# Filtered spectrum sums and half copies over two frequency pairs at a time, in a newly searched order

## The chip, the cores and the metric

One core of one Trainium2 chip. The metric is the device time of one launch in microseconds (us), as the median of several runs. A ratio is the mean time of one kernel's fast runs over that of the other's fast runs of the same rounds, with a 95% interval, so it is not quite the ratio of the medians quoted beside it. The profile of a run gives a span (first to last instruction of the core) about 2 us shorter than its time. Differences under 0.5 us are read from the spans of all runs, not from the times.

## The reference, cut to what matters

```python
def reference(A_x, A_w_r, A_w_i, B_x, B_w_gate, B_w_up, B_w_down):
    xn = layernorm(A_x)                       # 2048 x 640
    y  = irfft2(rfft2(xn) * (A_w_r + 1j * A_w_i))
    g  = xn @ B_w_gate; u = xn @ B_w_up       # 640 -> 1536
    return A_x + y + (g * u) @ B_w_down       # 1536 -> 640
```

(B_x is not used.) Two independent branches are computed from the same normed input: a two-dimensional spectral filter, and a gated product. The second is mostly TensorE work; the first has much small work on VectorE and ScalarE.

## The kernel before

The kernel is a list of about a thousand tasks with what they read and write. A table found by a search (`_PLAN`) says for each task its place in the order, its engine, and its bank in PSUM. The engines then run their own lists, each in that fixed order, and wait on semaphores where a task needs another's result. Five parts matter here: `GU` (gate and up matmuls, five of 128x512 each) with its eviction `eG` and product `H`, and the steps `t = 0..15` of the filter, two frequencies in each:

```python
# C_t: forward product, TensorE, two PSUM banks. In the plan every C from C_1 on has banks 0 and 1.
# WM_t: multiply with the filter, VectorE, reads C's banks and frees them (4 x 256, 2 x 130 columns)
def em_sm(c, pb=pb, yr=yr):                       # SM_t: sums, VectorE
    pa_, pb_ = v_pr[:, pb, 0], v_pr[:, pb, 1]
    c.e.tensor_tensor(v_l[0:64, yr, :, 0, :], pa_[0:64], pb_[64:128], _OP.subtract)
    return c.e.tensor_tensor(v_l[64:128, yr, :, 0, :], pa_[64:128], pb_[0:64], _OP.add)
def em_ja(c, yr=yr):                              # JA_t, JB_t: half copies, VectorE or ScalarE
    return copy_on(c, v_l[0:64, yr, :, 1, :], v_l[64:128, yr, :, 0, :])
def em_jb(c, yr=yr):
    dst, src = v_l[64:128, yr, :, 1, :], v_l[0:64, yr, :, 0, :]
    ...                                           # the same with the sign turned
# IA_2t, IA_2t+1: inverse product, TensorE, reads v_l; eIA: its eviction
```

Before the filter steps the other half transform runs beside the first GUs; after them come `I` (second inverse transform), `V` (combining it, VectorE), `ACC` (down projection, 128x320 matmuls) and `IV` (the last transform, into ACC's bank). In what follows a "forward product" is a C, a "filter" a WM, an "inverse product" an IA.

## Time and profile before

| | before |
|---|---|
| time, first reading | 206.17 us (206.08 to 206.24) |
| time beside the changed kernel | 206.12 us |
| span in the profile | 204.0 us |
| busy: TensorE, VectorE, ScalarE | 195.5, 185.5, 134.9 us |
| middle stretch (73.0 to 136.2 us): VectorE busy | 60.7 of 63.2 us |

The lines behind it are shown in the prediction. One reading matters for all that follows: VectorE's busy time leaves 2.5 us of the middle stretch, but it has 180 instructions there, so this is 14 ns at each seam (the step from one instruction to the next). Its longest gap is 0.1 us, and its list of waits is empty: it never waits. A stretch in which an engine shows such seams only is filled by that engine.

### The profile page before, as it was taken

To read this page: it belongs to the slowest core of one execution; us is meant where nothing else is said; L and a number is where in the kernel's file an instruction comes from. 1 tells how busy PE (TensorE), PEld (TensorE's weight loads), DVE (VectorE), ACT (ScalarE), POOL (GpSimd) and SP (SyncE) were. 2 spreads that over 40 slices of the span, in tenths; PEclk is the share of its full clock that TensorE was granted. 3 is DMA by queue.
4 is the path that set the end of the run, shared out by engine and by line. 5 is a ranking of instruction groups with operands and counts; after the bars stand their busy time and mean duration, and the time that the engine had idled before them with its cause. 6 is when DMAs were issued, how large, how long until landed. Compare 5 with 4: busy or idle time off the path is not lost.

```text
span 204.0 us, 4331 instructions
## 1 busy us (share of the span) xinstructions
PE 195.5 (96%) x1623; PEld 123.4 (60%) x1623; DVE 185.5 (91%) x430; ACT 134.9 (66%) x297; POOL 22.9 (11%) x53
## 2 busy tenths in 40 slices
PE   7999999999999999989898988989999999999995
PEld 7898545455454554554454445467666777777774
DVE  3799999999999999999999999998999988989823
ACT  3288999989965799888989896677314414041331
POOL 0000000000000023433250423530000000000000
PEclk9999999999999999999999999999999999999999
DMA  6999956455049143142542320025002413315432
GB/s 185 304 335 385 373 66 129 120 123 131 16 86 332 45 101 92 46 125 52 146 115 62 86 67 0 0 62 166 3 0 69 124 35 96 96 35 158 133 100 64
DMA packets 29668, 23.79 MB, mean 117 GB/s; under 512 B 10576, under 2 KB 27600, under 8 KB 29520
## 3 DMA queue, kind: packets, MB, share of 16 engines
q1 hardware_dynamic: 28848, 23.16, 40.8%
q10 hardware_dynamic: 800, 0.36, 0.6%
q8 instruction: 13, 0.21, 0.5%
q14 instruction: 7, 0.06, 0.1%
HBM read 18.92 MB, written 2.62 MB: 106 GB/s over the span
## 4 chain that ended last, share of the span: by engine, by line
PE 67%; DVE 27%; issue 3%; POOL 1%; ACT 0%; POOLq 0%; DVEq 0%
PE ps L1222 26%; PE ps L951 24%; DVE arena L1065 10%; PE ps L971 7%; DVE arena L688 4%; DVE arena L987 3%; DVE arena L1071 3%; DVE arena L1081 3%; DVE arena L1080 3%; PE ps L911 2%; PE ps L1145 2%; PE ps L723 2%; PE ps L1234 2%; DVE arena L1092 2%; PE ps L821 1%
## 5 line engine op out<-in xcount | busy, mean ns | idle before, releaser
L687 ACT ACTIVATE arena<-ps 64x321 bf16<-64x321 f32 (+7 forms) x241 | 114.6, 522 | 57.6 <-PE ps L1234 30.2
L951 PE MATMUL ps<-arena 128*128 128x512 bf16 x420 | 98.8, 379 | 0.9 <-DVE arena L987 0.9
L951 PEld LDWEIGHTS ps<-arena 128*128 128x128 bf16 x420 | 38.4, 97 | 41.3 <-ACT arena L687 2.6
L1222 PE MATMUL ps<-arena 128*128 128x320 bf16 (+2 forms) x396 | 57.1, 295 | 0.0
L1222 PEld LDWEIGHTS ps<-arena 128*128 128x128 bf16 x396 | 37.7, 98 | 13.7
L1065 DVE TENSOR_TENSOR arena<-ps,arena 128x256 bf16<-128x256 f32 x64 | 22.6, 416 | 0.4
L1100 POOL COPY arena<-arena 128x126 bf16<-128x126 bf16 x16 | 6.5, 404 | 112.2 <-DVE arena L1071 112.2
L987 DVE TENSOR_TENSOR arena<-arena 128x512 bf16<-128x512 bf16 x42 | 17.7, 422 | 0.6
L971 PE MATMUL ps<-arena 128*128 128x128 bf16 (+1 forms) x160 | 14.0, 246 | 0.3 <-ACT arena L778 0.3
L971 PEld LDWEIGHTS ps<-arena 128*128 128x128 bf16 x160 | 12.2, 98 | 1.5 <-issue 0.4
L1261 DVE TENSOR_TENSOR arena<-arena 128x640 bf16<-128x640 bf16 x15 | 7.2, 486 | 5.8 <-ACT arena L687 5.7
L1114 PEld LDWEIGHTS ps<-arena 128*128 128x128 bf16 x128 | 7.8, 119 | 5.6 <-ACT arena L687 2.3
L1102 POOL TENSOR_SCALAR arena<-arena 128x130 bf16<-128x130 bf16 x16 | 10.8, 674 | 0.0
L1114 PE MATMUL ps<-arena 128*128 128x64 bf16 x128 | 8.5, 198 | 1.3 <-POOL arena L1102 0.6
L1028 PEld LDWEIGHTS ps<-arena 128*128 128x128 bf16 x160 | 7.0, 98 | 4.2 <-DVE arena L688 0.9
L1048 PE MATMUL ps<-arena 128*128 128x321 bf16 x32 | 7.0, 301 | 2.5 <-DVE arena L1071 2.5
L688 DVE CAST arena<-ps 128x512 bf16<-128x512 f32 (+3 forms) x15 | 8.7, 609 | 0.2
L750 ACT ACTIVATE arena<-arena 128x640 bf16<-128x640 bf16 x10 | 8.4, 838 | 0.1
L1234 PE MATMUL ps<-arena 128*128 128x320 bf16 (+2 forms) x33 | 8.4, 295 | 0.0
L1028 PE MATMUL ps<-arena 128*128 128x64 bf16 (+1 forms) x160 | 8.0, 193 | 0.1
L1071 DVE TENSOR_TENSOR arena<-ps,arena 128x130 bf16<-128x130 f32 x32 | 8.0, 292 | 0.0
L863 DVE TENSOR_TENSOR arena<-arena 128x768 f32<-128x768 bf16 (+1 forms) x10 | 7.9, 788 | 0.0
(66 smaller groups left out, 211.3 us busy)
## 6 DMA issues: line engine op xcount, KB each, us to landing
arena<-in_A_x_dram SPq DMA_DIRECT2D x20, 160.0 KB, 2.5
arena<-in_A_w_r_dram SPq DMA_DIRECT2D x30, 80.2 KB, 2.2
arena<-in_A_w_i_dram SPq DMA_DIRECT2D x30, 80.2 KB, 2.2
out_dram<-arena SPq DMA_DIRECT2D x15, 160.0 KB, 1.8
arena<-in_B_w_gate_dram SPq DMA_DIRECT2D x4, 320.0 KB, 5.4
arena<-in_A_x_dram SPq DMA_DIRECT2D x1, 1280.0 KB, 10.0
arena<-c_tf SPq DMA_DIRECT2D x4, 256.0 KB, 10.2
arena<-c_ti SPq DMA_DIRECT2D x2, 512.0 KB, 4.9
```

What stands on the lines that cost most here:

```text
L687: return c.e.activation(dst, src, _ACTF.Copy)
L688: return c.e.tensor_copy(dst, src)
L951: ins = c.e.matmul(ps[:, bk, :], v_gw[:, w, j, ft, :], v_xt[:, j, rows], start=(j == 0), stop=(j == 4))
L971: ins = c.e.matmul(ps[:, bk, w * n:(w + 1) * n], v_gw[:, w, j, ft, :], v_xt[:, j, rows], start=(j == 0), stop=(j == 4))
L987: return c.e.tensor_tensor(v_ht[:, ft0, rows], v_gbf[:, rr, 0, :], v_gbf[:, rr, 1, :], _OP.mult)
L1028: ins = c.e.matmul(ps[:, bk, k * 64:k * 64 + n], v_uq[:, k, t, :], v_fd[:, k * 128 + w * n: k * 128 + w * n + n], start=True, stop=True)
L1065: c.e.tensor_tensor(dst, xh, wv, _OP.mult)
L1071: ins = c.e.tensor_tensor(d5[w], ps[:, bk:bk + 2, 256:321], wt[:, w, :, 0:321:5], _OP.mult)
L1102: return c.e.tensor_scalar(yg[:, :, 128:193], yg[:, :, 256:321], -1.0, None, _OP.mult)
L1114: c.e.matmul(ps[:, bk, 64 * k:64 * k + 64], yl[:, k:512:4], v_ti[:, q, 0, :], start=True, stop=True)
L1222: ins = c.e.matmul(ps[:, bk, 0:sl3.stop - sl3.start], v_ht[:, ft, a * 128:(a + 1) * 128], v_wd[:, ft, sl3], start=(ft == _FT_ORDER[0]), st ...
L1234: return c.e.matmul(ps[:, bank_of(own), 0:sl3.stop - sl3.start], v_sm[:, 2, :], v_v[:, a, sl3], start=False, stop=True)
```

## The change

The intent is to halve the number of small VectorE instructions: sums and half copies are made over two steps (four frequencies) at once, so that the fixed cost of an instruction is paid half as often. The planner's durations for these tasks were set higher, and the whole order was searched again. The core of the diff (the plan, all of whose lines change, is cut):

```diff
-        b_pr = alloc("PR", 2 * 1024)
-        b_l = alloc("L", _NY * 1024)
+        b_pr = alloc("PR", 2048)
+        b_l = alloc("L", 2 * 2048)
...
-            wm = T("WM_%d" % t, "dve", 4 * _d_dve(256) + 2 * _d_dve(130), em_wm,
+            wm = T("WM_%d" % t, "dve", 1862.0, em_wm,
...
+            if t % 2 == 0:
+                continue
+            lr = (t // 2) % 2
+            def em_sm(c, lr=lr):
+                pa_, pb_ = v_pr[:, 0], v_pr[:, 1]
+                c.e.tensor_tensor(v_l[0:64, lr, :, 0, :], pa_[0:64], pb_[64:128], _OP.subtract)
+                return c.e.tensor_tensor(v_l[64:128, lr, :, 0, :], pa_[64:128], pb_[0:64], _OP.add)
...
-            for g in range(2):
-                q = 2 * t + g
+            for q in range(2 * t - 2, 2 * t + 2):
```

## The prediction

> **What bounds the kernel now.** I read the page first, then the chain of waits in order of time, then the busy times of each engine over three stretches, then the groups of instructions with shapes kept apart, and last the waits of the middle stretch.
>
> The page says that two engines are nearly full all the time, and where each of them is not.
>
> ```profile
> PE 195.5 (96%) x1623; PEld 123.4 (60%) x1623; DVE 185.5 (91%) x430; ACT 134.9 (66%) x297; POOL 22.9 (11%) x53
> PE   7999999999999999989898988989999999999995
> DVE  3799999999999999999999999998999988989823
> ACT  3288999989965799888989896677314414041331
> ```
>
> TensorE drops to 8 in slices 17 to 25 only, that is from about 80 to 130 us. In that region the chain of waits leaves TensorE and stays on VectorE:
>
> ```profile
> 70.63 0.59 PE ps L1028 x15
> ...
> 73.03 1.32 DVE arena L1065 x4
> 74.35 0.42 DVE arena L1071 x2
> 74.77 0.34 DVE arena L987
> 75.13 0.42 DVE arena L1080
> 75.57 0.42 DVE arena L1081
> 76.02 1.42 DVE arena L1065 x4
> 77.44 0.43 DVE arena L1071 x2
> 77.88 0.29 DVE arena L688
> 78.20 0.30 DVE arena L1092
> ```
>
> The reader is to see one task after the other with no hole: the filter products of one pair of frequencies (L1065 four times, L1071 twice, 1.85 us together), a gated product (L987), the sums (L1080 and L1081, each 0.44 us from start to start), and the two half copies (L688 and L1092, 0.32 us from start to start). This goes on until 135.5 us. Before 73 and after 136 the chain is TensorE alone.
>
> ```profile
> 1.04:73.03 71.99, 71.71 (x549) 44.24 (x550) 68.31 (x156) 58.26 (x129) 0.00 (x0) 1.00 0.69 190
> 73.03:136.23 63.20, 58.34 (x548) 31.47 (x546) 60.70 (x180) 54.90 (x123) 22.59 (x48) 1.00 0.27 68
> 136.23:201.75 65.52, 65.48 (x534) 47.64 (x531) 56.02 (x95) 21.76 (x47) 0.00 (x0) 1.00 0.29 88
> ```
>
> The columns are the stretch, its length, then busy time of PE, PE weight load, DVE, ACT and POOL. Only in the middle one is TensorE open, for 4.9 us by this count. The count flatters it, since matmul spans overlap. Worked out from distances in the trace (five 128x512 matmuls take 1.08 us, fifteen of L1028 take 0.59, a group of six of L1114 and L1116 takes 0.20, a 320-column one 0.136), the middle holds 190 x 0.216 + 135 x 0.039 + 32 x 0.20 + 30 x 0.136 = 56.8 us of streaming in 63.2 us: 6.4 us open. The last stretch by the same count holds 65.3 us in 65.5.
>
> So the most that a change of the middle stage can give is about 6.4 us, 3.1% of 206.17.
>
> **What the Trainium skill says.** "VectorE: DVE Perf Modes", section "The TRN2 errata", says that an instruction from SBUF pays a fixed latency once, however large it is. Its section "Side-by-side: where the cycles go" gives two 16-bit elements a cycle to a two-source operation and four to a copy, at 0.96 GHz: 0.52 and 0.26 ns an element. The trace agrees roughly:
>
> ```profile
> L987 DVE TENSOR_TENSOR arena<-arena 128x512 bf16<-128x512 bf16 x42 | 17.7, 422 | 0.6
> L988 DVE TENSOR_TENSOR arena<-arena 128x256 bf16<-128x256 bf16 x4 | 1.1, 270 | 0.0
> L1261 DVE TENSOR_TENSOR arena<-arena 128x640 bf16<-128x640 bf16 x15 | 7.2, 486 | 5.8 <-ACT arena L687 5.7
> L688 DVE COPY arena<-arena 64x512 bf16<-64x512 bf16 x14 | 4.2, 299 | 0.4
> ```
>
> From 256 to 512 elements is 152 ns (0.59 each), from 512 to 640 is 64 ns (0.50); some 150 ns is fixed. "TensorE: Matmul & The Clock Gate", section "Back-to-back issue gap", gives N/2.4 + 2.5 ns, 216 at 512, which is the distance above; the 131 ns that it also gives does not occur here. "Perfetto Trace Analysis", section "Identifying the Most-Contended Engine", warns that matmul busy time is no measure of headroom; here it reads 58.3 where the streaming is 56.8.
>
> **The change part by part.** I call the work of two frequencies a step; the stage has 16.
>
> Sums. Before: 32 instructions of 512 elements at 0.44 us, 14.1 us. After: 16 of 1024. One should last 422 + 512 x 0.55 = 0.70 us, 0.72 from start to start: 11.5 us. Saved: 2.6 us.
>
> Half copies. Before, 27 on VectorE at 0.32 us (8.6 us) and 5 on ScalarE at 0.63. After, the order of instructions shows 13 on VectorE and 3 on ScalarE. One on VectorE should last 299 + 512 x 0.26 = 0.43, 0.45 with its gap: 5.9 us. Saved: 2.7 us. The three on ScalarE should take about 1.05 each (the 512-element one takes 0.63; I add the page's rate of 0.83 ns per element), 3.2 us as before.
>
> Filter products: unchanged, 16 x 1.85 = 29.6 us.
>
> Moved by the new order: in the stage VectorE gets two more evictions of 320 columns (+1.0), one more gated product (+0.44), and loses one double eviction of 64x321 (-1.0). Net +0.4.
>
> VectorE in the stage: 62.5 - 2.6 - 2.7 + 0.4 = 57.6 us. Had TensorE room, this would be the gain: 5 us.
>
> TensorE's work is the same in kind and number, only in another order. Between the first L1048 and the end of the inverse transforms the new order has 205 gate and up matmuls of 512 where the old one had 190, and 10 of the down projection where it had none: 56.8 + 15 x 0.216 + 10 x 0.136 = 61.4 us. So the author knew that VectorE no longer fills the stage and put TensorE work there that was done later; the last stretch falls from 65.3 to about 60 us of streaming. ScalarE: five more 512-column evictions at some 0.55 and one less of 320, so 54.9 + 2.3 = 57.2 us.
>
> The stage therefore has 61.4 us on TensorE, 57.6 on VectorE, 57 on ScalarE. TensorE becomes the bound, and the gain is 6.4 us less what stays open on it. In the stretch up to 73 us three engines are as full (71.7, 68.3 and 58.3 of 72.0) and TensorE keeps no hole, so a good order can do it. In the stage the waits go round a loop (evict, transform, filter, sum, copy, transform back, evict), so I expect 2.3 us to stay open, under 4%. The last stretch gets tight: by my count from the rows of before, the first combined group of the inverse is ready about 14.3 us after the last inverse transform, and TensorE arrives at its first use at 13.9 to 14.3; the third is ready at 38.1 against 38.0 to 38.4. I take off 0.6 us for that and for the seams. Gain: 6.4 - 2.3 - 0.6 = 3.5 us, so 202.6 us.
>
> **The rivals.** First, a wait for four spectra takes the place of the wait for two. The inverse transform of a step now waits for the filter of the next one, one sum and two copies: 1.85 + 1.44 + 0.9 = 4.2 us later at worst. If TensorE has too little other work in its fixed order, or the buffer of the fifth products (three deep, held longer) stalls the filter, the stage keeps 4 to 6 us open and the gain is 0 to 2 us: 204 to 206. Against it: the order puts 3 to 5 us of TensorE work behind each last forward product, and 5 us behind the very last.
>
> Second, VectorE's gain comes out whole and TensorE keeps under 1 us open, as in the first stretch: 200.7 to 201.5. For it speaks that six waits fall away: of the old chain 2.5 us are TensorE's forward product waiting for the filter to give its two banks back, since all steps after the first used the same pair of banks, and the new order spreads them over four pairs.
>
> ```profile
> PE ps L1048 <- DVE arena L1071: 2.5, 7, 0.6
> PEld ps L1114 <- ACT arena L687: 2.3, 4, 0.7
> ```
>
> Third, ScalarE becomes the bound, at 57 of some 63 us with evictions that hold banks: its row of the second line above shows 2.3 us of TensorE waiting for it already. If that doubles, the time is about 204.
>
> **Range and chances.** The middle of the three is 202.6. Two us open less gives 201, two more gives 204.4; I take 201.0 to 204.4 for 8 in 10. Faster by over 2% needs 202.05, a gain of 4.1 of the possible 6.4 us, so under 2.3 us lost in all: 0.36. Slower by 2% would need a deadlock-like stall in every step: 0.02. The rest, 0.62, is within 2%.
>
> **What would show it right or wrong.** Right: the sums at 0.69 to 0.72 us and 16 of them, the copies at 0.42 to 0.45, the chain of the middle no longer VectorE without a break but mixed with long runs of L951; TensorE's open time there down from 6.4 to 2 to 3 us; the first and last stretches without new holes. Wrong: sums over 0.8 us; TensorE waiting over 4 us for ScalarE, POOL or the copies in the middle; or a last stretch in which TensorE waits for the combining of the inverse.

## The result, and the profile after

The changed kernel takes 199.44 us (199.32 to 200.22, 4 runs) against 206.12 us (205.89 to 206.24): ratio 0.9685, interval 0.9659 to 0.9711. The gain is 6.7 us, 3.2%. It is below the predicted range, and above what the prediction held to be possible.

First the page of the changed kernel: its summary line, then the busy tenths of three engines in 40 slices.

```profile
PE 192.8 (98%) x1623; PEld 123.5 (63%) x1623; DVE 177.8 (90%) x396; ACT 138.0 (70%) x299; POOL 28.4 (14%) x53
PE   7999999999999999999999999999999999999995
DVE  3799999999999989999898998995999999989753
ACT  3378999999965789999999999966414342335220
```

All of TensorE's eights are gone; in the middle it is now VectorE that has some, and ScalarE is at nine from slice 15 to 25 (counted from 0). Next the three stretches, cut at the first filter instruction and at the modelled end of the last inverse product, 0.16 us after the next matmul has started (columns as before: length, then PE, weight load, DVE, ACT, POOL).

```profile
1.04:74.45 73.41, 72.77 (x556) 45.18 (x557) 69.11 (x156) 59.91 (x131) 0.00 (x0) 1.00 0.69 187
74.45:135.09 60.64, 60.17 (x572) 33.82 (x570) 55.82 (x150) 56.24 (x124) 28.15 (x48) 1.00 0.27 70
135.09:194.97 59.88, 59.81 (x499) 44.51 (x497) 52.45 (x90) 21.83 (x46) 0.00 (x0) 1.00 0.31 95
```

The middle is only 2.6 us shorter, but it holds more: 572 matmuls where there were 548, and the last stretch has 499 instead of 534. The gain is a sum of both, and a ledger that needs only the distances of two matmul shapes shows it. I cut at the start of the first forward product and at the end of the last inverse product. The old middle runs from 72.44 to 136.23 (63.79 us), the new from 73.40 to 134.93 (61.53 us), with 15 more 128x512 matmuls (0.216 us each) and 10 more of 320 columns (0.136), 4.6 us. So the middle gained 63.79 - 61.53 + 4.6 = 6.9 us. The first stretch has five 512-column matmuls more (1.08 us) and is 0.96 longer: 0.1 gained. The last has 20 and 10 fewer (5.67 us) and is 65.52 - 60.04 = 5.48 shorter: 0.2 lost. The sum is 6.8 us, the difference of the spans.

The chain of waits of the changed kernel, in the middle, is TensorE going from task to task:

```profile
103.88 0.27 PE ps L1045 x2
104.15 1.08 PE ps L948 x5
105.43 0.15 PE ps L1025 x5
105.57 1.08 PE ps L948 x5
106.85 0.27 PE ps L1045 x2
107.12 0.30 PE ps L1025 x5
```

The groups by shape show the new instructions (partitions x elements, count, busy us, mean ns):

```profile
L1089 DVE TENSOR_TENSOR arena<-arena 64x1024 bf16<-64x1024 bf16 x8 | 5.5, 688 | 0.3
L1101 DVE TENSOR_SCALAR arena<-arena 64x1024 bf16<-64x1024 bf16 x8 | 3.4, 422 | 0.3
L684 ACT ACTIVATE arena<-arena 64x1024 bf16<-64x1024 bf16 x3 | 3.2, 1051 | 0.0
```

Sums 0.69, copies 0.42, a copy on ScalarE 1.05 us: all as predicted. Of the waits of the middle, those that touch the forward product (L1045 now) and the filter (L1062) are down to one line, the first, and it is VectorE that waits; the second is one of TensorE's longest waits that are left (us in total, times, longest):

```profile
DVE arena L1062 <- PE ps L1045: 1.0, 2, 0.7
PEld ps L948 <- ACT arena L684: 0.8, 3, 0.4
```

The 2.5 us in which TensorE's forward product waited for the previous filter are gone: in the new plan ten of the fifteen forward products after the first have other banks than the one before (x7 tests what this is worth).

### The profile page after: what moved, and what is told of

Read it like the earlier page. It is cut to its first block, busy times and chain, and to the rows that moved or that the text cites. A ratio compares the mean times of both kernels' runs of the same rounds, so it can differ in the third digit from the quotient of the medians.

```text
span 197.2 us, 4300 instructions
## 1 busy us (share of the span) xinstructions
PE 192.8 (98%) x1623; PEld 123.5 (63%) x1623; DVE 177.8 (90%) x396; ACT 138.0 (70%) x299; POOL 28.4 (14%) x53
## 4 chain that ended last, share of the span: by engine, by line
PE 72%; ACT 13%; DVE 5%; SPq 4%; DMA 4%; issue 1%
PE ps L948 33%; PE ps L1224 26%; ACT arena L684 7%; SPq L678 4%; DMA arena<-in_A_x_dram 4%; ACT arena L747 3%; ACT arena L738 3%; PE ps L1147 2%; PE ps L1236 2%; PE ps L1116 2%; PE ps L1025 2%; PE ps L1045 2%; PE ps L908 2%; DVE arena L1062 1%; DVE arena L685 1%; PE ps L1118 1%
## 5 line engine op out<-in xcount | busy, mean ns | idle before, releaser
L684 ACT ACTIVATE arena<-ps 128x512 bf16<-128x512 f32 (+6 forms) x245 | 118.5, 525 | 49.5 <-PE ps L1236 21.1
L948 PE MATMUL ps<-arena 128*128 128x512 bf16 x420 | 97.5, 379 | 0.3 <-ACT arena L684 0.2
L1224 PE MATMUL ps<-arena 128*128 128x320 bf16 (+2 forms) x396 | 57.2, 295 | 0.0
L1077 POOL COPY arena<-arena 128x126 bf16<-128x126 bf16 x16 | 9.3, 582 | 104.4 <-DVE arena L1068 104.4
L1062 DVE TENSOR_TENSOR arena<-ps,arena 128x256 bf16<-128x256 f32 x64 | 22.6, 416 | 1.5 <-PE ps L1045 1.0
L968 PE MATMUL ps<-arena 128*128 128x128 bf16 (+1 forms) x160 | 13.9, 246 | 0.4 <-issue 0.3
L1079 POOL TENSOR_SCALAR arena<-arena 128x130 bf16<-128x130 bf16 x16 | 11.7, 728 | 0.0
L1025 PE MATMUL ps<-arena 128*128 128x64 bf16 (+1 forms) x160 | 8.7, 193 | 0.3 <-ACT arena L684 0.3
L1078 POOL COPY arena<-arena 128x126 bf16<-128x126 bf16 x16 | 8.6, 538 | 0.0
L1236 PE MATMUL ps<-arena 128*128 128x320 bf16 (+2 forms) x33 | 7.6, 295 | 0.0
```

What stands on the lines that cost most here:

```text
L684: return c.e.activation(dst, src, _ACTF.Copy)
L948: ins = c.e.matmul(ps[:, bk, :], v_gw[:, w, j, ft, :], v_xt[:, j, rows], start=(j == 0), stop=(j == 4))
L968: ins = c.e.matmul(ps[:, bk, w * n:(w + 1) * n], v_gw[:, w, j, ft, :], v_xt[:, j, rows], start=(j == 0), stop=(j == 4))
L1025: ins = c.e.matmul(ps[:, bk, k * 64:k * 64 + n], v_uq[:, k, t, :], v_fd[:, k * 128 + w * n: k * 128 + w * n + n], start=True, stop=True)
L1062: c.e.tensor_tensor(dst, xh, wv, _OP.mult)
L1079: return c.e.tensor_scalar(yg[:, :, 128:193], yg[:, :, 256:321], -1.0, None, _OP.mult)
```

## The experiments

The theories were V: the time of VectorE's instructions in the middle was what the change bought, and O: the newly searched order bought it. The prediction rested on V, checked by O's list of TensorE work. There were seventeen runs, all timed (x16 is x3's file and x17 the changed kernel, once more); the medians are to be read against 199.44 to 199.59 for the changed kernel and 206.04 to 206.25 for the one before.

### x1, x2, x3: the new order with the old lengths

```diff
-    c.e.tensor_tensor(v_l[0:64, lr, :, 0, :], pa_[0:64], pb_[64:128], _OP.subtract)
-    return c.e.tensor_tensor(v_l[64:128, lr, :, 0, :], pa_[64:128], pb_[0:64], _OP.add)
+    for h in (slice(0, 2), slice(2, 4)):
+        c.e.tensor_tensor(v_l[0:64, lr, h, 0, :], pa_[0:64, h], pb_[64:128, h], _OP.subtract)
+        ins = c.e.tensor_tensor(v_l[64:128, lr, h, 0, :], pa_[64:128, h], pb_[0:64, h], _OP.add)
+    return ins
```

The copies are split in the same way (x1 both, x2 the sums, x3 the copies).

> The changed kernel with its order, buffers and waits, but each sum and each half copy issued as two instructions of half the length, as the kernel before had them. This gives VectorE about 16 x 0.17 + 13 x 0.19 = 5.2 us back in the middle stage. Theory V (VectorE's time in the middle was the bound, and the longer instructions took it away): the stage is VectorE-bound again, 202 to 203.5 us, and TensorE's waits come back. Theory O (the newly searched order made the gain, whatever the instructions last): within 0.7 us of 199.4.

> Only the sums split: +2.7 us on VectorE. Theory V, with some 2 to 3 us that VectorE stands idle in the changed kernel's middle stage: 199.6 to 200.8 us. Theory O: 199.2 to 199.8.

> Only the half copies split: +2.5 us on VectorE and +0.6 us on ScalarE. Theory V: 199.6 to 200.8 us, about as the split sums. Theory O: 199.2 to 199.8.

Measured: x1 199.61 us (ratio 0.9681, 0.9667 to 0.9695), x2 199.61 (0.9678), x3 199.08 (0.9657). Theory V, as stated, fell: with the order in place the longer instructions are worth 0.2 us by the times and 0.5 us by the spans (mean 197.75 us for x1, 197.28 for the changed kernel), and the halved sums alone 0.3 (x2, 197.60). The halved copies cost nothing (x3, 197.27). The middle of x1, from first filter instruction to last inverse product:

```profile
74.15:135.37 61.22, 60.63 (x570) 34.04 (x568) 58.69 (x178) 56.54 (x127) 22.94 (x48) 1.00 0.26 69
```

VectorE leaves 2.5 us in 178 instructions; of these 0.7 us are two waits for TensorE, 0.5 of it at the very end, and the rest are seams of about 10 ns. So x1 all but fills VectorE again, and TensorE is full as well. From the first forward product the middle of x1 takes 62.28 us, 0.75 more than the changed kernel's, of which 0.3 was made good by an earlier start; the old order needed 63.79 us for 4.6 us less TensorE work. One thing keeps x1 from being the old lengths in full: the two halves of a copy stand in one task with no wait between them, and such a pair costs less than two tasks did.

```profile
86.94 0.50 DVE L685 COPY arena<-arena 64x512 bf16<-64x512 bf16 x2
87.47 0.49 DVE L1107 TENSOR_SCALAR arena<-arena 64x512 bf16<-64x512 bf16 x2
```

That is 0.53 us from start to start for two, where the kernel before took 2 x 0.32. VectorE's busy time in x1's middle is 3.0 us above the changed kernel's, not the 5.2 us that I had reckoned, and still 2.0 below the 60.7 us of the kernel before.

### x4: the longer instructions in the old order

The old lists of every engine were kept, the sums and copies of even steps left out, and the inverse products of even steps moved behind the copies of the odd step, as they must be.

> The longer instructions in the old order, changed only where it must be (the sums and copies of even steps leave, their inverse transforms move behind the copies of the odd step; 29 PSUM banks change). Theory V: most of the gain is there without the search, 200.5 to 203 us. Theory O: little gain or a loss, 204.5 us or more, since TensorE meets inverse transforms that are not ready.

Measured: 218.42 us, ratio 1.0603 (1.0558 to 1.0648), a loss as theory O expected. Its waits say why:

```profile
DVE arena L1062 <- PE ps L1045: 15.1, 14, 2.4
```

VectorE's filter waits 15.1 us for forward products. In the old order these stand behind inverse products that now come later. So the lengths without a new order lose 12 us. This is one hand-made order, not the best for these tasks, and it says only that the change could not be had without the search.

### x5, x6: less TensorE work in each kernel

```diff
-                        for j in range(5):
+                        nj = 4 if rows.start == 1536 and ft < 9 else 5
+                        for j in range(nj):
```

> The kernel before with 18 of its 128x512 matmuls left out in the middle stage (the last of five accumulation steps of the gate and up products of the last quarter of the rows, 9 of 12 column blocks; wrong result on purpose): 3.9 us less on TensorE. If VectorE is the bound of that stage: 205.3 to 206.2 us. If TensorE is: 202.2 to 202.8.

> The same 18 matmuls left out of the changed kernel. If TensorE is now the bound and VectorE and ScalarE have 2 to 4 us left: 195.5 to 197.5 us. If the other engines are as close as TensorE: 198.5 to 199.4.

Measured: x5 206.18 us (ratio 1.0003, 0.9986 to 1.0020), x6 198.81 us (0.9646, 0.9630 to 0.9662). The result is no longer the reference's sum, though its error stayed within the tolerance. In the old kernel 3.9 us of TensorE work in the middle cost nothing at all: TensorE waits instead. The middle of x5, the same window as before:

```profile
73.03:136.23 63.20, 54.24 (x513) 29.70 (x521) 60.70 (x180) 55.14 (x123) 22.54 (x48) 1.00 0.27 68
```

VectorE's 60.70 us is the number of the kernel before to the last digit, TensorE's is 4.1 less. In the changed kernel the same cut gives 0.6 us (0.7 by the spans), the second of the two expectations and not the 2 to 4 us of the first: TensorE is not the only bound there.

### x7, x10: the forward product waits for the previous filter

```diff
-                   prio=pq, bank="pair", cls="b")
+                   prio=pq, bank="pair", cls="b", after=[wm] if t else ())
```

> The changed kernel in which each forward product of a step also waits for the filter of the step before, as it did in the kernel before, where all used one pair of PSUM banks. Same order and banks. If the spreading over banks is a part of the gain: 200.4 to 202 us. If not: within 0.5 us of 199.4.

> The changed kernel with both the forward product's wait for the previous filter and the sums and copies in halves. If the two effects add: 199.4 + 2.5 + 0.2 = 202.1 us. If the shorter instructions matter only where the forward product waits for the filter, as in the kernel before: 203.5 to 206 us.

Measured: x7 201.89 us (ratio 0.9796), x10, with x1's halves, 203.01 us (0.9851, 0.9834 to 0.9868), between its two expectations. In x7 the forward product waits for the filter again:

```profile
PE ps L1045 <- DVE arena L1068: 1.9, 2, 1.5
```

The wait costs 2.4 us, and with it the old lengths cost 1.1 us instead of 0.2 (1.5 instead of 0.5 by the spans). So the two parts are not independent: VectorE's time matters more where TensorE cannot run ahead of the filter.

### x9: the promised VectorE time, in the old order

```diff
+            nh = 256 if t < 3 else 128
-                c.e.tensor_tensor(v_l[0:64, yr, :, 0, :], pa_[0:64], pb_[64:128], _OP.subtract)
+                c.e.tensor_tensor(v_l[0:64, yr, :, 0, 0:nh], pa_[0:64], pb_[64:128], _OP.subtract)
```

(The other sum and VectorE's copies likewise; the result is wrong.)

> The kernel before, order and waits untouched, with the sums and VectorE's half copies from the fourth step on only half as long (wrong result on purpose). That takes about 13 x 2 x 0.14 + 23 x 0.065 = 5.2 us from VectorE in the middle stage, as much as the change promised. If VectorE's time is what bounds the old order: 201 to 202 us. If the old order's waits bound it: 204 us or more.

Measured: 201.27 us, ratio 0.9761 (0.9742 to 0.9780), 4.9 us less for some 5.2 us of VectorE time. Its middle, cut as in the ledger, takes 131.75 - 72.74 = 59.0 us, 4.8 less than before. So V holds in the old order, nearly one for one. It was not wrong about the kernel before; it was wrong to carry the sum over to the new order.

### x8, x11, x12: half copies between ScalarE and VectorE

The engine in the plan is changed: in x8 the five of one sign that VectorE does go to ScalarE; in x11 the three that ScalarE does go to VectorE; x12 is x11 with copies in halves. (In this cut and the next, tasks stand under their names; the plan has their numbers.)

```diff
-    (JA, 2, -1)      # engine 2 is VectorE; in x11 and x12: 1 -> 2
+    (JA, 1, -1)      # engine 1 is ScalarE
```

> The five half copies of one sign that VectorE does go to ScalarE too: +5.3 us there, -2.2 us on VectorE. If ScalarE is close behind TensorE (it stands idle 4.4 us of the stage): 200 to 201.5 us. If it is not: within 0.5 us of 199.4.

> The three half copies that ScalarE has in the changed kernel go to VectorE: -3.2 us on ScalarE, +1.3 us on VectorE. If ScalarE is the next bound, as its great loss in the opposite run says: 198.5 to 199.2 us. If not: 199.3 to 200.

> As the run with all copies on VectorE, and the copies in two halves each, which read 199.08 us alone. Candidate for the best version: 198.4 to 199.2 us; no better than 199.1 if neither helps.

Measured: x8 207.04 us (ratio 1.0050), x11 199.74 us (0.9698), x12 199.87 us (0.9697). x8 is a miss, at 200 to 201.5 expected: more work for ScalarE costs 7.6 us, more than the work itself (5.3). Some 1.4 us of this is a lost clock: after TensorE had waited 2.6 us for ScalarE, ten matmuls of 512 columns took 3.57 us from the first start to the end of their turn, instead of 2.16. The rest I put down to waits that spread through the fixed order; it was not taken apart. Less work for ScalarE gives nothing, but in x11 VectorE has 1.3 us more in exchange. With x1 and x6 this says what the changed kernel's middle is: TensorE, VectorE and ScalarE all within a few us of it. Relief of TensorE gives 0.6 us and relief of ScalarE at VectorE's cost nothing; relief of VectorE alone was not tried.

### x13, x14, x15: which property of the new order

In x13 three GUs (15 matmuls of 128x512) and two pieces of ACC (10 of 128x320) were moved behind the last inverse products, their evictions on ScalarE with them. In x14 the kernel before keeps its lists, but PSUM banks in the middle are given out by longest free, and no forward product takes the banks of the last. x15 is x13 with x10's two edits.

```diff
 # x13, TensorE's list at the end of the middle
-    C_15 GU_11_12_1 GU_11_12_0 IA_27 ACC_1_1_0 IA_26 GU_10_12_0 ACC_0_0_0 IA_28 IA_30 IA_31 IA_29
+    C_15 IA_27 IA_26 IA_28 IA_30 IA_31 IA_29 GU_11_12_1 GU_11_12_0 ACC_1_1_0 GU_10_12_0 ACC_0_0_0
```

> The changed kernel with three groups of gate and up matmuls (15 of 128x512) and two of the down projection (10 of 128x320) moved from before the last inverse transforms to behind them, their evictions with them. They are 15 x 0.216 + 10 x 0.136 = 4.6 us of TensorE. If the gain is TensorE work put where TensorE had to wait: 202.4 to 204 us. If it only stands in another place: under 200.2.

> The kernel before with the same order on every engine, but in the middle stage the PSUM bank that has been free longest is given out, and no forward product takes the banks of the one before it (86 banks change). If the old order is held by VectorE's time alone: 205.5 to 206.5 us. If it is held by the single pair of banks: 203 to 204.7.

> The new order with all three taken back: the late place of the 25 matmuls, the forward product's wait for the previous filter, and sums and copies in halves. If the three are the account of the change and add: 206 to 207.5 us. If they overlap: 203 to 205.5.

Measured: x13 205.44 us (ratio 0.9959, 0.9936 to 0.9982), x14 209.96 us (1.0209), x15 209.70 us (1.0171). All three are above their expectations. x13 shows a second cost beside the 4.6 us. Its page (busy tenths and granted clock), then two lines of TensorE's timeline (start, length, what, idle before):

```profile
PE   7899999999999999999999999479999999999995
PEclk9999999999999999999999999958999999999999
```

```profile
133.40 0.38 PE L1116 MATMUL ps<-arena 128*128 128x64 bf16 x4 [2.84 <-issue]
135.06 4.04 PE L948 MATMUL ps<-arena 128*128 128x512 bf16 x9 [0.22 <-issue]
```

TensorE stands still for 2.8 us while VectorE finishes the last two steps, and after that nine matmuls take 4.04 us, about 0.43 each instead of 0.216, because the granted clock has halved. Over the run it is 0.983. So x13 shows that the moved work filled a hole: the middle without its 4.6 us lasts 61.67 us, some 0.5 of it for the lost clock, where it lasted 61.53 with it. The 6.0 us are the hole and the lost clock. From the starts I estimate the lost clock at 2.5 us of the profiled run's 6.4 (1.9 in the nine matmuls, 0.6 in the small ones around them), which leaves about 3.9 us for the place of the work. x15 has the same clock (0.984), adds up to more than the whole change, and so is no closed account.

x14 is a miss: spreading the banks by a simple rule makes the old order 3.9 us slower. (Its profile is of the slowest of its four runs, 211.74 us, which also has a stretch at half clock; the other three, at full clock, agree on 209.9 to 210.0.) Its waits show new ones on ScalarE (TensorE's forward product waits 4.0 us for it, against none before), as banks now go to whatever ScalarE has not yet evicted. That the spreading is a gain is shown for the new order only (x7).

### x16, x17: is there a better version?

> The half copies in two halves each, timed again beside the changed kernel. If the 0.36 us of the first reading were real: 199.0 to 199.2 us and 0.3 us or more below the other run. If noise: within 0.2 us of it.

> The changed kernel itself, unaltered, as the other side of that comparison: 199.3 to 199.6 us.

Measured on one chip in the same rounds: x16 (the file of x3) 199.08 us (199.00 to 199.18; ratio 0.9651, 0.9638 to 0.9664), x17 199.59 us (199.17 to 199.94; 0.9677, 0.9660 to 0.9694). The copies in two halves read 0.3% faster twice, but not by their work: the spans of the four runs of x16 average 197.22 us and those of the five of x17 197.32, and TensorE's middle takes 61.53 us in x3 as in the changed kernel. The difference lies outside the span, where the profile shows nothing, and its cause stays open. As a schedule neither is better.

## Why the prediction was wrong, point by point

- **What bounds the middle: right.** x5 and x9 show it: TensorE's relief is worth nothing there, VectorE's is worth 4.9 of 5.2 us. Two readings of the lines were off and changed nothing: TensorE's eights lie in slices 17 to 26, which is 87 to 138 us; and "this goes on until 135.5 us" holds for VectorE's work, but the chain goes over to GpSimd at 130.67, whose last instruction ends at 135.7 us.
- **The costs of the new instructions: right.** 0.69 against 0.70 for a sum, 0.42 against 0.43 for a copy, 1.05 for one on ScalarE (the trace has its rate: an eviction takes it 598 ns at 512 columns and 435 at 320, 0.85 ns a column). VectorE in the middle: predicted 57.6 us; measured, 55.7 busy with 149 seams of 14 ns, 57.8. ScalarE: predicted 57.2, measured 56.2.
- **"So the most that a change of the middle stage can give is about 6.4 us": mis-sized.** The term "135 x 0.039" was taken from "fifteen of L1028 take 0.59", a piece of the chain that counts up to the modelled end of the last one, when the next matmul has long started. By the starts the same fifteen take 0.44 (70.62 to 71.06), 0.029 each, as five in 0.15 do in the changed kernel. So the middle held 55.5 us of streaming and 7.7 were open. This is 1.3 us of the miss. (The count also takes in matmuls that only reach into the cut; by the starts inside it 8.2 were open.)
- **"I expect 2.3 us to stay open, under 4%": this failed most.** With 203 matmuls of 128x512 and 11 of 320 columns, and the same others, the new middle streams 203 x 0.216 + 135 x 0.029 + 32 x 0.20 + 30 x 0.136 + 11 x 0.136 = 59.7 us in the 60.5 from 74.45 to 134.93: 0.8 us are open, 1.5 fewer (1.3 by the starts inside the cut). The prediction held against it that "the waits go round a loop"; but in the new order no forward product waits for the filter. The prediction had seen this: its second rival names the 2.5 us of that wait and the four pairs of banks. It did not ask what the wait costs (x7: 2.4 us), and so gave the rival too little weight. That rival was the better guide, though with the short ceiling its 200.7 to 201.5 us was still too slow.
- **"I take off 0.6 us for that and for the seams": not needed.** TensorE reached the first use of the combined inverse at 149.03, 14.1 us after the last inverse product (13.9 to 14.3 were reckoned), and did not wait: VectorE had it ready at 148.80. The last stretch lost 0.2 us.
- **"TensorE becomes the bound": half right.** It is full, but 3.9 us taken from it give 0.6 (x6).
- **The unasked question.** The prediction took the gain as bought by VectorE's shorter instructions and only limited by TensorE. The new order gives nearly all of it even with the old lengths: x1 has VectorE all but filled, with 2.0 us less work than before, and still takes 199.61 us. VectorE's time and the order are two ways to the same 7 us of open TensorE, and their effects overlap rather than add.

What stays open: how much of the gain a search on the old tasks would have found. x1 makes it likely to be most, but x1 still groups two steps in a task. One rival was neither tested nor named: the first search worked with VectorE durations that were too short. The scheduling code in the two kernel files, run on the host without the chip, gives the old order 196.3 us with its own durations and 203.5 with the measured ones (filter 1.86, two sums 0.88, half copy 0.32, and for GpSimd's task the new file's 1.18); the profile says 204.0. It gives the new order 197.0, and the profile says 197.2. So the old order was chosen for a VectorE that is faster than the real one, and true durations alone, with the old tasks, might have bought much of the gain. And how the 6.9 us of the middle divide between filling and spreading: for the spreading x7 gives 2.4; for the filling x13 gives 6.0 with a lost clock in it, about 3.9 by my estimate without.

## What to carry to other kernels

Where an engine that is full all the time else has holes in one stage, count the holes from the starts of its instructions in runs without any wait, and count them as the prize: here the new order took 6.9 of about 8 us. A stage that VectorE fills can hold extra TensorE work for nothing (x5 and x13: some 4 us taken out of it made it hardly shorter), so ask what later work could be moved into it before asking how to make VectorE's instructions cheaper. In a static schedule, which PSUM banks a product gets decides whether TensorE may run ahead, and a change of task shapes without a new order can lose more than it wins. Where a planner made the order, compare its durations with the profile first, and replay its plan with the measured ones: here this gives both kernels to 0.5 us.

## What the Trainium skill lacked or had wrong

- "TensorE: Matmul & The Clock Gate", section "What's actually happening": it puts the return to the slow clock after an idle window of about 3.4 us. In x13 a hole of 2.84 us, after one of 0.88 with about 0.5 us of matmuls between them, was enough; matmuls of 512 columns then took 0.43 us for about 4 us. In x8 a single hole of 2.60 us was enough, and TensorE was busy for 1.36 of the 3.42 us before the clock fell (columns as before, then granted clock, DMA share and GB/s):

```profile
92.90:96.32 3.42, 1.36 (x15) 0.65 (x11) 2.58 (x7) 1.50 (x3) 2.22 (x3) 1.00 0.33 80
96.32:99.73 3.41, 2.87 (x7) 1.04 (x8) 0.85 (x2) 2.15 (x5) 0.00 (x0) 0.50 0.46 115
```

- "VectorE: DVE Perf Modes", section "The DRAIN you can't avoid": it says that leaving the semaphores out between copies saves nothing, though the same section also says that an instruction that is not held (not made to wait for all earlier ones) starts earlier, without a figure. Here two copies of 64x512 with no wait between them took 0.53 us from start to start, and two in tasks of their own, with waits, 0.64; a filter's four products of 416 ns each took 1.42 us together.
- No page that I read says what a hole in TensorE is worth where another engine fills the stage: here 3.9 us of matmuls were free (x5).
